# Attention and two feed-forward layers on one core: matmul kinds priced in the list schedule, a list of priority shifts, first loads in parts, TensorE warmed

## The chip, the cores and the metric

The kernel runs on one core of a Trainium2 chip. The metric is the time of one execution on the device in microseconds (us). It is a single program: all inputs come from HBM and the result goes back to HBM.

## What is computed

```python
# B, H, S, D = 4, 8, 576, 64
scores = q @ k^T / sqrt(D), causal mask, softmax    # per batch b and head h
local  = softmax @ v
q_p    = where(q > 0, q, exp(q) - 1) + 1
mem    = (q_p @ M_prev) / (q_p @ z_prev + 1e-6)
x      = g * mem + (1 - g) * local                  # g = sigmoid(beta) per head
x      = x as [2304 tokens, 512]
y      = (s * relu(x @ w_in)**2 + b) @ w_out        # first layers,  512 -> 2048 -> 512
h      = y @ w_in2                                  # second layers, 512 -> 2048 -> 512
out    = (max(h, 0) + alpha * min(h, 0)) @ w_out2
```

## The kernel before

The program is not written in the order in which it runs. `build` records operations (`op`): an engine, an estimated duration, the keys that it reads and writes, a priority, and a function that issues its instructions. `Plan.order` then makes a list schedule: it walks a model of the engines in time, and on each engine, when it is free, it takes the ready operation with the smallest priority number. The instructions are issued in that order, and each engine runs its own in order. The estimates therefore decide only the order; the waits on the chip are the real ones. Some operations (kind "x", in `either`) may go to ScalarE or to VectorE; the schedule gives them to the one that is free first.

The work has three parts. **Attention** goes by batch `b` and by pair of heads `p`: loads of q, k and v (`features` L526, `pair` L662, `values` L483), a feature map of q (L528, L529 on ScalarE, L532 on VectorE), matmuls with the memory (L549, normalised by L555 to L559), scores (L796), their row maximum (`largest`, L769, VectorE), exponentials (`exps`, L762, ScalarE), a scaling of the weights (batch 0: L579 on ScalarE or L581 on VectorE; later batches L630 and L634), a transposition (batch 0: on TensorE, L594, copied back by L602 on ScalarE or L604 on VectorE; later by DMA), and the outputs (L684, L700). The result of batch 0 is split into a high and a low part (L723 on ScalarE, L725 on VectorE), which the first layers read. `allone`, a tile of ones, is the weight of a small summing matmul (L499).

**The first layers** (`moe`) go by blocks of tokens, 512 in the first and 256 in the others, and by 16 slices `f` of the hidden width. `g1` makes one slice of the hidden layer in the bank `hb` with 12 matmuls (L928 to L930); ScalarE empties the bank (L941), squares (L942) and rounds (L943), VectorE makes the low part (L944), and `g2` multiplies with `w_out` (12 matmuls, L962 to L964). The weights of each slice are made while block 0 runs: a load (L880), three operations of VectorE (L882, L885, L888), a copy (L891) and a subtraction (L894). Batches 1 to 3 of the attention are interleaved with these layers.

**The second layers** (`hidden`, `output`) run when the attention is over: rows of matmuls of 384 columns (L1241 to L1243 and L1373 to L1375). At the very end `join` (L1256) adds the last bank to a kept part, and one DMA (L1389) stores 384 columns.

TensorE's matmuls have kinds: scores, turning (L594), outputs, memory, sum (L499) and layers. The schedule before adds 130 ns where a layer follows something else and 90 ns where something else follows a layer:

```python
layer = prio >= 10 ** 7
dur += 0 if layer == self.layer else 130.0 if layer else 90.0
```

All loads and stores are issued by SyncE's queue (SPq in the rows), in program order.

Of the kernel before, what the change touches and what calls it, by code (L numbers as in the profile page):

```python
# [20 lines left out]
NBIG, NB = 512, 256  # L21
NS, NTH = 384, NT // 2
# [36 lines left out]
KG = 1  # L59
# [5 lines left out]
WP = 1.7  # L65
TICK, WARM = 3413.3, 1275.0
# [19 lines left out]
class Plan:  # L86
# [8 lines left out]
    def __init__(self, nslots, nextra):  # L95
        self.nextra = nextra
        self.lean = 0
        self.ops = []
        self.ways = {}
        self.writer = {}  # L100
        self.readers = {}
        self.nslots = nslots
        self.layer = False

    def op(self, eng, dur, fn, r=(), w=(), prio=None, bytes_=0, claim=()):
# [16 lines left out]
        for k in list(r) + list(w):  # L122
            s = k[0] if isinstance(k, tuple) else k
            if isinstance(s, Slot) and s not in slots:
                slots.append(s)
                s.left += 1
        self.ops.append((eng, dur, fn, deps | late, i + self.lean if prio is None else prio, bytes_, slots, late, claim))
# [9 lines left out]
    def order(self):  # L137
        n = len(self.ops)
        left = [len(o[3]) for o in self.ops]
# [60 lines left out]
        gone = set()  # L200
        while len(out) < n:
# [88 lines left out]

def t_r(n):
    return 115.5 if n <= NB else (n + 32) / 2.4
# [31 lines left out]
def build(tc, kp, vd, qp, mzd, beta8, sb2, win1, wout1, win2, wout2, alpha, outT):  # L324
# [8 lines left out]
    with tc.tile_pool(name="sb", bufs=1) as sb, tc.tile_pool(  # L333
# [102 lines left out]
        def consts2():  # L436
# [6 lines left out]
        op("POOL", 200, lambda: nc.gpsimd.memset(allone, 1.0), w=["allone"])  # L443
        op("POOL", 200, lambda: nc.gpsimd.memset(ident, 1.0), w=["ident"])
        op("POOL", 500, lambda: nc.gpsimd.affine_select(
            out=ident, in_=ident, pattern=[[-1, 128]], compare_op=ALU.is_equal, fill=0.0, base=0, channel_multiplier=1),
           r=["ident"], w=["ident"])

# [7 lines left out]
        def bank_at(bk):  # L456
            return banks[bk.place - NSLOT - 3 * XF]

# [19 lines left out]
        def values(b, p, u, gs):  # L478
# [5 lines left out]
               r=gate(b, u, KV), prio=-7 if b + p == 0 else None, w=[sv], bytes_=512 * n)  # L484
# [9 lines left out]
            def part(x):  # L494
# [5 lines left out]
               r=[("tot", j), "allone"], w=[bk], prio=ATT + cnt["ch"] * 10 - 6)  # L500
# [15 lines left out]
        def features(b, p, u, gs):  # L516
# [4 lines left out]
            def cols(s):  # L521
# [945 lines left out]
```

## Time and profile before

| | |
|---|---|
| median of 3 runs | 937.06 us (937.0 to 938.16) |
| profiled execution, its time | 939.22 us |
| its span, first to last instruction | 937.2 us |
| TensorE busy | 921.1 us, 98% of the span |
| VectorE busy | 717.4 us, 77% |
| ScalarE busy | 604.6 us, 65% |

The span is that of the profiled execution, which lasted 2.0 us longer than its span. Busy time is a sum over the whole span; the stages differ, so the shares are read stage by stage. Matmuls overlap each other: the time from the start of one to the start of the next says more than the length of one.

### The profile page before, as it was taken

What the parts mean: (1) busy time and instruction counts of PE and PEld (TensorE: products, weight loads), DVE (VectorE), ACT (ScalarE), POOL (GpSimd) and SP (SyncE); (2) the same over time, 40 slices, a digit from 0 to 9 for tenths busy, and PEclk for the clock granted to TensorE, in tenths of its full rate; (3) what the DMA queues carried; (4) which work ended last, traced back from release to release, by engine and by line L of the source; (5) the groups of instructions that cost most, each with busy time, mean ns of one, the idle gap of its engine ahead of it and who ended that gap; (6) DMA issues with size and microseconds to landing.
All of it is one profiled execution on the core that took longest, in us unless ns stands there. A gap on an engine that the chain in (4) does not pass through costs nothing.

```text
span 937.2 us, 19293 instructions
## 1 busy us (share of the span) xinstructions
PE 921.1 (98%) x7164; PEld 845.2 (90%) x7164; DVE 717.4 (77%) x1636; ACT 604.6 (65%) x1413; POOL 5.3 (1%) x29
## 2 busy tenths in 40 slices
PE   7999999999999999999999999999999999999998
PEld 5677777688888888999999999999999999999998
DVE  6999998857777776647778767859568889786874
ACT  7887757767888888744544479748457665454452
POOL 1000000000000000000000000000000000000000
PEclk9999999999999999999999999999999999999999
DMA  4358955466766575567967746635348793725301
GB/s 158 98 144 254 284 180 166 124 139 128 183 146 148 121 168 109 90 185 253 323 228 281 257 156 218 210 111 165 115 133 271 231 306 117 238 68 163 107 1 68
DMA packets 154094, 160.43 MB, mean 171 GB/s; under 512 B 86928, under 2 KB 127888, under 8 KB 154000
## 3 DMA queue, kind: packets, MB, share of 16 engines
q1 hardware_dynamic: 154000, 159.20, 57.4%
q8 instruction: 56, 0.92, 0.4%
q14 instruction: 38, 0.31, 0.1%
HBM read 92.84 MB, written 46.66 MB: 149 GB/s over the span
## 4 chain that ended last, share of the span: by engine, by line
PE 83%; DVE 10%; ACT 3%; issue 2%; DMA 2%; SPq 0%; DVEq 0%; ACTq 0%
PE yb L962 6%; PE yb L964 6%; PE hb L928 6%; PE yb L963 6%; PE hb L929 6%; PE hb L930 6%; PE yb L1373 3%; PE sp L1374 3%; PE yb L1374 3%; PE sp L1373 3%; PE yb L1375 3%; PE sp L1375 3%; PE yb L1241 3%; PE yb L1243 3%; PE yb L1242 3%; PE sp L1243 2%
## 5 line engine op out<-in xcount | busy, mean ns | idle before, releaser
L962 PE MATMUL yb<-gr,wt 128*128 128x256 f32 (+2 forms) x512 | 154.5, 302 | 0.8 <-ACT gr L943 0.5
L928 PE MATMUL hb<-xr,wt 128*128 128x256 f32 (+1 forms) x512 | 152.9, 299 | 2.3 <-ACT gt L941 2.2
L964 PE MATMUL yb<-gr,wt 128*128 128x256 f32 (+2 forms) x512 | 151.5, 296 | 0.8 <-DVE gr L944 0.5
L930 PE MATMUL hb<-xr,wt 128*128 128x256 f32 (+1 forms) x512 | 149.7, 292 | 0.3 <-DVE wt L894 0.3
L929 PE MATMUL hb<-xr,wt 128*128 128x256 f32 (+1 forms) x512 | 149.7, 292 | 0.0
L941 ACT ACTIVATE gt<-hb 128x256 f32<-128x256 f32 (+1 forms) x128 | 52.3, 408 | 91.4 <-PE hb L930 76.9
L928 PEld LDWEIGHTS hb<-xr,wt 128*128 128x128 f32 x512 | 96.3, 188 | 11.3 <-issue 4.4
L962 PEld LDWEIGHTS yb<-gr,wt 128*128 128x128 f32 x512 | 96.3, 188 | 9.2 <-issue 3.7
L944 DVE TENSOR_TENSOR gr<-gt,gr 128x256 fp32r<-128x256 f32 (+1 forms) x128 | 58.3, 456 | 58.9 <-ACT gr L943 56.7
L964 PEld LDWEIGHTS yb<-gr,wt 128*128 128x128 f32 x512 | 96.9, 189 | 5.7 <-DVE gr L944 2.8
L930 PEld LDWEIGHTS hb<-xr,wt 128*128 128x128 f32 x512 | 96.7, 189 | 3.5 <-DVE wt L894 0.9
L929 PEld LDWEIGHTS hb<-xr,wt 128*128 128x128 f32 x512 | 96.3, 188 | 2.1
L963 PE MATMUL yb<-gr,wt 128*128 128x256 f32 (+2 forms) x320 | 93.8, 293 | 0.0
L963 PEld LDWEIGHTS yb<-gr,wt 128*128 128x128 f32 x320 | 60.3, 188 | 1.2
L943 ACT CAST gr<-gt 128x256 fp32r<-128x256 f32 (+1 forms) x128 | 55.3, 432 | 6.8 <-PE yb L963 4.4
L942 ACT ACTIVATE gt<-gt 128x256 f32<-128x256 f32 (+1 forms) x128 | 56.9, 445 | 2.8
L963 PE MATMUL yb<-gr,wu 128*128 128x256 f32 (+2 forms) x192 | 56.3, 293 | 0.0
L1198 ACT CAST xr<-spare 128x768 fp32r<-128x768 f32 x37 | 30.9, 836 | 26.6 <-PE sp L1374 10.1
L1267 ACT ACTIVATE waste<-poolx 128x384 f32<-128x384 f32 x48 | 25.2, 526 | 29.2 <-DVE poolx L1256 28.5
L1199 DVE TENSOR_TENSOR xr<-spare,xr 128x768 fp32r<-128x768 f32 x37 | 35.3, 955 | 9.6 <-ACT xr L1198 9.4
L963 PEld LDWEIGHTS yb<-gr,wu 128*128 128x128 f32 x192 | 36.1, 188 | 0.8
L1112 DVE TENSOR_TENSOR wp<-poolx,wp 128x768 fp32r<-128x768 f32 (+1 forms) x32 | 25.9, 822 | 8.9 <-ACT wp L1110 8.1
(505 smaller groups left out, 2570.2 us busy)
## 6 DMA issues: line engine op xcount, KB each, us to landing
g<-poolx SPq DMA_DIRECT2D x96, 192.0 KB, 1.9
poolu<-g SPq DMA_DIRECT2D x30, 384.0 KB, 4.2
room<-wout SPq DMA_DIRECT2D x14, 512.0 KB, 4.1
room<-win SPq DMA_DIRECT2D x13, 512.0 KB, 3.9
pool<-win SPq DMA_DIRECT2D x12, 512.0 KB, 4.6
pool<-wout SPq DMA_DIRECT2D x12, 512.0 KB, 5.0
spare<-y SPq DMA_DIRECT2D x12, 384.0 KB, 3.7
spare<-g SPq DMA_DIRECT2D x12, 384.0 KB, 3.6
```

What stands on the lines that cost most here:

```text
L928: T.matmul(H_, W_h, X_h, start=(d == 0), stop=False)
L929: T.matmul(H_, W_h, X_l, start=False, stop=False)
L930: T.matmul(H_, W_l, X_h, start=False, stop=(d == KD - 1))
L942: op("ACT", t_act(n), lambda: A.activation(out=t_, in_=t_, func=AF.Square), w=[tk], prio=-1)
L943: op("ACT", t_act(n), lambda: A.copy(out=G_h, in_=t_), r=[tk], w=[("gh", gj)], prio=-1)
L944: op("DVE", t_dve(n), lambda: V.tensor_tensor(out=G_l, in0=t_, in1=G_h.bitcast(F32), op=ALU.subtract), r=[tk, ("gh", gj)], w=[("gl", gj)], ...
L962: T.matmul(Y, W_h, G_h, start=first, stop=False, skip_group_check=True)
L963: T.matmul(Y, W_l, G_h, start=False, stop=False, skip_group_check=True)
L964: T.matmul(Y, W_h, G_l, start=False, stop=False, skip_group_check=True)
L1373: T.matmul(o, W_h, G_h, start=(m == e == 0 and P in (1, 2, 4, 5)), stop=False, skip_group_check=True)
L1374: T.matmul(o, W_l, G_h, start=False, stop=False, skip_group_check=True)
L1375: T.matmul(o, W_h, G_l, start=False, stop=False, skip_group_check=True)
```

## The change

Five edits. (1) Each TensorE operation now carries its kind, and `change` gives the price of each pair of kinds in the schedule's model, in place of the two numbers above. (2) `NUDGE`, a table of some 250 operations, shifts their priorities. (3) q and k of the first pair are loaded in two parts each (256 and 320 columns of q, 384 and 192 of k); the order of the first loads becomes q, k, q, k, beta, memory, v, where it was q, k, v, beta, memory. (4) `allone` is filled by VectorE at the start, and six matmuls of `allone` with itself run on TensorE before any load has landed (`begin`). (5) The last sum of the program is made and stored in two halves of 192 columns, one stored by SyncE's queue and one by ScalarE's.

```diff
+FIRST = 256, 384
+BEGIN = 6
+NUDGE = {
+    6: -10, 14: -16, 25: -2, 36: -437, 52: -1, 85: 27, 121: 5, 122: 5, 123: 5, 124: 9, 125: 5, 126: 5, 127: 5,
...
+    3340: 184, 3341: -1, 3392: 5, 3399: -36, 3433: -114, 3461: 1, 3473: -169, 3727: 282,
+}
...
     def order(self):
         n = len(self.ops)
+        for i, shift in NUDGE.items():
+            o = self.ops[i]
+            self.ops[i] = (*o[:4], o[4] + shift, *o[5:])
...
             if e == "PE":
-                layer = prio >= 10 ** 7
-                dur += 0 if layer == self.layer else 130.0 if layer else 90.0
-                self.layer = layer
+                dur += change(kind, self.kinds[i])
+                kind = self.kinds[i]
...
+def change(a, b):
+
+    if a is None:
+        return 0
+    if a == "scores":
+        return -89 if b == a else 0
+    if b == "scores":
+        return {"layers": 95, "outputs": 40}.get(a, 100)
+    if a == "outputs":
+        return {"layers": 75, "sum": 40, "outputs": 100}.get(b, 168)
+    if a == "sum":
+        return 140
+    return {"outputs": 9, "sum": 20}.get(b, 0) if a == "layers" else 0
...
 def t_r(n):
-    return 115.5 if n <= NB else (n + 32) / 2.4
+    return 116.4 if n <= NB else (n + 32) / 2.4
...
-        op("POOL", 200, lambda: nc.gpsimd.memset(allone, 1.0), w=["allone"])
+        op("DVE", 200, lambda: V.memset(allone, 1.0), w=["allone"], prio=-9)
+        bk0 = bank_for(0)
+
+        def begin():
+            for _ in range(BEGIN):
+                T.matmul(bank_at(bk0)[:, 0:128], allone, allone, start=True, stop=True)
+
+        op("PE", BEGIN * 4 * 128 / 2.4, begin, r=["allone"], w=[bk0], prio=-20, kind="memory")
...
-               r=gate(b, u, KV), prio=-7 if b + p == 0 else None, w=[sv], bytes_=512 * n)
+               r=gate(b, u, KV), prio=-5 if b + p == 0 else None, w=[sv], bytes_=512 * n)
...
-            op("SP", 475, lambda: nc.sync.dma_start(out=cols(sq), in_=qp[b, p][:, x0:x1_]),
-               r=gate(b, u, KV), prio=-9 if b + p == 0 else None, w=[sq], bytes_=512 * nx)
-            op("ACT", t_act(nx), lambda: A.activation(out=cols(se), in_=cols(sq), func=AF.Exp), r=[sq], w=[se])
+            for k, a, z in ((0, x0, FIRST[0]), (1, FIRST[0], x1_)) if b + p == 0 else ((0, x0, x1_),):
+                op("SP", 475, lambda a=a, z=z: nc.sync.dma_start(out=at(sq, S)[:, a:z], in_=qp[b, p][:, a:z]),
+                   r=gate(b, u, KV), prio=3 * k - 12 if b + p == 0 else None, w=[(sq, "b") if k else sq], bytes_=512 * (z - a))
+            op("ACT", t_act(nx), lambda: A.activation(out=cols(se), in_=cols(sq), func=AF.Exp), r=[sq, (sq, "b")], w=[se])
...
-            op("SP", 475, lambda: nc.sync.dma_start(out=at(sk, nkeys), in_=kp[b, p][:, 0:nkeys]),
-               r=gate(b, u, KG), prio=-8 if b + p == 0 else None, w=[sk], bytes_=512 * nkeys)
+            for k, a, z in ((0, 0, FIRST[1]), (1, FIRST[1], nkeys)) if b + p == 0 else ((0, 0, nkeys),):
+                op("SP", 475, lambda a=a, z=z: nc.sync.dma_start(out=at(sk, nkeys)[:, a:z], in_=kp[b, p][:, a:z]),
+                   r=gate(b, u, KG), prio=3 * k - 11 if b + p == 0 else None, w=[(sk, "b") if k else sk], bytes_=512 * (z - a))
...
-                    op("PE", t_p([y[6] for y in todo[::2]]), mm, r=[sqp, sk], w=keys + room_for, prio=ATT + (base + 2 * step[0]) * 10)
+                    op("PE", t_p([y[6] for y in todo[::2]]), mm, r=[sqp, sk] + [(s, "b") for s in (sqp, sk) if max(step) > 1],
+                       w=keys + room_for, prio=ATT + (base + 2 * step[0]) * 10, kind="scores")
...
+                                if (b, P, j) == (NTH // NS - 1, 2, 1):
+                                    for h, dma in enumerate((nc.sync, nc.scalar)):
+                                        x, n, c = NS // 2 * h, NS // 2, buf()
+
+                                        def add(c=c, x=x, n=n, k=kept[part, j]):
+                                            V.tensor_tensor(out=see(c, F32, 0, n), in0=bank_of[bank[1]][:, x:x + n],
+                                                            in1=see(k, F32, x, n), op=ALU.add)
+
+                                        act(c, t_dve(n), add, r=[bank[j]] + kept[part, j].keys, prio=-1, eng="DVE")
+                                        op(("SP", "ACT")[h], 475, lambda c=c, x=x + tq, n=n, d=d, dma=dma: dma.dma_start(
+                                            out=outT[:, d, x:x + n], in_=see(c, F32, 0, n)), r=c.keys, bytes_=512 * n)
+                                    continue
```

The edits move instructions on every engine from the first one on. Three places show how. The line numbers of the changed kernel are higher: its scores are L847 (L796 before), its maxima L820 (L769), its features L582 (L532), its constants L479 to L481 (L437 to L439), its layers L980 to L982 and L1014 to L1016 (L928 to L930 and L962 to L964).

The first place is the start of VectorE's stream. Before, the features of q and the three constants made from beta (`wsc`, `wlc`, `bgc`) stand ahead of the first maximum:

```order
L532 SCALAR_TENSOR_TENSOR room_73<-room_73,room_72 128x576
L437 TENSOR_SCALAR wsc<-wsc 128x36
L438 TENSOR_SCALAR wlc<-wsc 128x36
L439 TENSOR_SCALAR bgc<-bgc 128x36
L769 ISA sp_106,mx<-sp_106,mask 128x256
L769 ISA mx 128x1
L769 ISA sp_107,mx<-sp_107,mask 128x256
L769 ISA mx 128x1
L555 SCALAR_TENSOR_TENSOR nrm<-yb_101,bgc 128x4
```

In the changed kernel VectorE begins with the tile of ones and takes one maximum ahead of the features:

```order
L495 MEMSET allone 128x128
L820 ISA sp_107,mx<-sp_107,mask 128x256
L820 ISA mx 128x1
L582 SCALAR_TENSOR_TENSOR room_72<-room_72,room_71 128x576
L479 TENSOR_SCALAR wsc<-wsc 128x36
L480 TENSOR_SCALAR wlc<-wsc 128x36
L481 TENSOR_SCALAR bgc<-bgc 128x36
L820 ISA ob,mx<-ob,mask 128x256
L820 ISA mx 128x1
L820 ISA hb,mx<-hb,mask 128x384
L820 ISA mx 128x1
```

One maximum has moved ahead of the features and the constants, and the normalisation of the memory's result (L555 before) has moved behind further maxima.

The second place is on TensorE where the first layers begin, from the last group of slice f=0 (weights `wt_481`) to the first of slice f=1 (`wt_792`). Before, nothing stands between them:

```order
L928 MATMUL hb<-xr,wt_481 128x512
L929 MATMUL hb<-xr,wt_481 128x512
L930 MATMUL hb<-xr,wt_481 128x512
L928 MATMUL hb<-xr,wt_792 128x512
L929 MATMUL hb<-xr,wt_792 128x512
L930 MATMUL hb<-xr,wt_792 128x512
```

In the changed kernel (`wt_489`, then `wt_687`) a pair of scores of the attention stands between the two slices:

```order
L548 MATMUL sp_107<-vsc,allone 128x1
L980 MATMUL hb<-xr,wt_489 128x512
L981 MATMUL hb<-xr,wt_489 128x512
L982 MATMUL hb<-xr,wt_489 128x512
L847 MATMUL sp_106<-pool 128x384
L847 MATMUL ob<-pool 128x384
L980 MATMUL hb<-xr,wt_687 128x512
L981 MATMUL hb<-xr,wt_687 128x512
```

The scores moved to where the bank `hb` changes hands from one slice to the next.

The third place is on TensorE at the turn from block 0 to block 1, where the last `g2` of block 0 is followed by slice f=1 of block 1 (256 columns). Before, again nothing stands between:

```order
L962 MATMUL yb_104<-gr,wt_1759 128x512
L963 MATMUL yb_104<-gr,wt_1759 128x512
L964 MATMUL yb_104<-gr,wt_1759 128x512
L928 MATMUL hb<-xr,wt_792 128x256
L929 MATMUL hb<-xr,wt_792 128x256
L930 MATMUL hb<-xr,wt_792 128x256
```

In the changed kernel a pair of scores stands there:

```order
L1014 MATMUL yb_104<-gr,wt_1746 128x512
L1015 MATMUL yb_104<-gr,wt_1746 128x512
L1016 MATMUL yb_104<-gr,wt_1746 128x512
L847 MATMUL ob<-pool,poolx 128x512
L847 MATMUL sp_106<-pool,poolx 128x512
L980 MATMUL hb<-xr,wt_687 128x256
L981 MATMUL hb<-xr,wt_687 128x256
L982 MATMUL hb<-xr,wt_687 128x256
```

Counted over TensorE's whole stream, the runs of one kind are 189 before and 188 in the changed kernel, and the runs of layers among them 70 and 70.

## Rows read from the trace of the kernel before

**Rows 1.** Busy time by stage: length, busy us of each engine, PEclk, DMA.

```profile
0.00:4.57 4.57, 0.00 (x0) 0.03 (x1) 0.00 (x0) 2.13 (x3) 2.74 (x16) 1.00 0.59 192
4.57:16.00 11.43, 10.80 (x58) 7.29 (x60) 8.59 (x35) 7.80 (x25) 0.00 (x0) 1.00 0.60 204
16.00:64.00 48.00, 46.41 (x463) 34.00 (x464) 46.89 (x184) 44.26 (x143) 0.15 (x1) 1.00 0.32 103
64.00:176.00 112.00, 109.10 (x647) 81.42 (x646) 104.86 (x254) 75.94 (x165) 0.20 (x1) 1.00 0.72 208
176.00:560.00 384.00, 381.16 (x3779) 349.87 (x3779) 270.44 (x758) 257.27 (x698) 2.25 (x11) 1.00 0.66 181
560.00:933.70 373.70, 373.67 (x2224) 372.62 (x2222) 286.04 (x410) 217.19 (x384) 0.00 (x0) 1.00 0.49 158
933.70:937.20 3.50, 0.00 (x0) 0.00 (x0) 0.56 (x1) 0.00 (x0) 0.00 (x0) 0.88 0.31 112
```

**Rows 2.** Waits of TensorE, whole span: total us, times, longest.

```profile
PE sp L796 <- DMA room<-kp: 4.6, 1, 4.6
PE hb L928 <- ACT gt L941: 2.2, 2, 1.5
PE sp L499 <- DVE pool L559: 0.6, 1, 0.6
```

**Rows 3.** Waits of VectorE from 0 to 64 us.

```profile
DVE room L532 <- ACT room L529: 5.0, 1, 5.0
DVE wsc L437 <- ACT wsc L433: 1.4, 1, 1.4
DVE nrm L555 <- PE yb L549: 0.5, 1, 0.5
```

**Rows 4.** Timeline of the first 16 us: start, us, engine, line.

```profile
0.80 0.39 SPq L526 DMA_DIRECT2D room<-qp  x1
1.25 0.42 SPq L662 DMA_DIRECT2D room<-kp  x1
...
3.72 0.68 ACT L528 ACTIVATE room<-room 128x576 f32<-128x576 f32 x1 [1.64 <-DMA room<-qp]
...
4.57 1.22 PE L796 MATMUL sp<-room 64*128 64x256 f32 x4 [4.57 <-DMA room<-kp]
...
7.60 0.42 DVE L769 CUSTOM_DVE_ANT_0 sp<-sp,mask 128x256 f32<-128x256 f32 x1
...
7.70 2.51 PE L549 MATMUL yb<-mz,room 128*128 128x130 f32 x10 [0.63 <-DVE bgc L439]
...
14.46 0.61 PE L549 MATMUL yb<-mz,room 128*128 128x130 f32 x4
```

**Rows 5.** Groups of VectorE by shape, 0 to 66 us: busy us, mean ns.

```profile
L581 DVE TENSOR_SCALAR room<-room,sm 128x384 f32<-128x384 f32 x7 | 2.6, 415 | 0.0
...
L604 DVE COPY room<-yb 128x256 f32<-128x256 f32 x3 | 1.2, 414 | 0.0
...
L604 DVE COPY room<-yb 128x512 f32<-128x512 f32 x1 | 0.7, 692 | 0.0
...
L885 DVE SCALAR_TENSOR_TENSOR room<-pool,room 128x512 int32<-128x512 int32 x1 | 0.7, 693 | 0.0
```

**Rows 6.** Timeline of TensorE at the turn from block 0 to block 1.

```profile
183.72 0.38 PE L928 MATMUL hb<-xr,wt 128*128 128x256 f32 x1 [1.52 <-ACT gt L941]
```

**Rows 7.** Timeline of TensorE where scores follow layers.

```profile
317.03 0.28 PE L963 MATMUL yb<-gr,wt 128*128 128x256 f32 x1
317.15 0.28 PE L964 MATMUL yb<-gr,wt 128*128 128x256 f32 x1
317.35 0.69 PE L796 MATMUL sp<-poolx,pool 64*128 64x512 f32 x1
```

**Rows 8.** The last sum, in the timeline.

```profile
933.70 0.56 DVE L1256 TENSOR_TENSOR waste<-hb,waste 128x384 f32<-128x384 f32 x1 [0.49 <-PE hb L1375]
```

**Rows 9.** DMA issues at the end: count, KB each, us from issue to landing.

```profile
out_t<-waste SPq DMA_DIRECT2D x1, 192.0 KB, 1.9
```

More of the change, by code (lines that the diff above doesn't have):

```diff
@@ L102, in __init__, with op @@
         self.nslots = nslots
-        self.layer = False
-    def op(self, eng, dur, fn, r=(), w=(), prio=None, bytes_=0, claim=()):
+        self.kinds = []
+    def op(self, eng, dur, fn, r=(), w=(), prio=None, bytes_=0, claim=(), kind=None):
         i = len(self.ops)
@@ L126, in op @@
                 s.left += 1
+        self.kinds.append(kind)
         self.ops.append((eng, dur, fn, deps | late, i + self.lean if prio is None else prio, bytes_, slots, late, claim))
@@ L200, in order @@
         gone = set()
+        kind = None
         while len(out) < n:
@@ L442, in build @@
         op("DVE", 200, consts2, r=["wsc", "bgc"], w=["wsc", "bgc"])
-        op("POOL", 200, lambda: nc.gpsimd.memset(allone, 1.0), w=["allone"])
[L444 to L447, printed above, removed]
         cnt = {"ch": 0}
@@ L457, in bank_at @@
             return banks[bk.place - NSLOT - 3 * XF]
+        op("DVE", 200, lambda: V.memset(allone, 1.0), w=["allone"], prio=-9)
[4 more added lines that the diff above has]
+        op("PE", BEGIN * 4 * 128 / 2.4, begin, r=["allone"], w=[bk0], prio=-20, kind="memory")
+        op("POOL", 200, lambda: nc.gpsimd.memset(ident, 1.0), w=["ident"])
+        op("POOL", 500, lambda: nc.gpsimd.affine_select(
+            out=ident, in_=ident, pattern=[[-1, 128]], compare_op=ALU.is_equal, fill=0.0, base=0, channel_multiplier=1),
+           r=["ident"], w=["ident"])
         def gate(b, u, ahead):
@@ L499, in values @@
             op("PE", 100, lambda: T.matmul(bank_at(bk)[:, 0:1], allone, tot, start=True, stop=True),
-               r=[("tot", j), "allone"], w=[bk], prio=ATT + cnt["ch"] * 10 - 6)
+               r=[("tot", j), "allone"], w=[bk], prio=ATT + cnt["ch"] * 10 - 6, kind="sum")
             op("DVE", 131, lambda: V.tensor_scalar(
@@ L552, in features @@
                 gk = "bgc" if b in WHOLE else ("gg", u % 2)
-                op("PE", n * t_f(MZ), mm, r=[se, "mz", gk], w=[bk], prio=ATT + cnt["ch"] * 10 - 5)
+                op("PE", n * t_f(MZ), mm, r=[se, "mz", gk], w=[bk], prio=ATT + cnt["ch"] * 10 - 5, kind="memory")
                 gg = (bgc[:, 9 * p:9 * p + 2] if b in WHOLE else vsc[:, u % 2, 4:6]).rearrange("p (o h) -> p o h", o=1).to_broadcast([128, n, 2])
@@ L594, in mm @@
                                 T.transpose(bank_at(bk)[:, 128 * i:128 * i + 128], p_c(128 * (k0 + i), 128), ident)
-                        op("PE", n * t_t(128), mm, r=wk + ["ident"], w=[bk], prio=ATT + ch * 10 + 1)
+                        op("PE", n * t_t(128), mm, r=wk + ["ident"], w=[bk], prio=ATT + ch * 10 + 1, kind="turning")
                         def p_t(k0, n=1, p_c=p_c):
@@ L706, in outputs @@
                    r=sum((turned[odd, c][0] for turned, c in every for odd in range(2)), []) + [(sa, g) for g, _, _, _ in sets] + [sv, "ident"],
-                   w=list(oks.values()), prio=ATT + sets[0][2] * 10 + 2)
+                   w=list(oks.values()), prio=ATT + sets[0][2] * 10 + 2, kind="outputs")
                 for g, cs, _, _ in sets:
@@ L934, in g1 @@
                     ks_ = [(x, s, e) for x in ("xh", "xl") for s in range(2) for e in range(KD)]
-                op("PE", 3 * t_r(n), mm, r=wkeys("wi", f) + ks_ + [("xset", xs)], w=["H"], prio=MOE + cm["m"])
+                op("PE", 3 * t_r(n), mm, r=wkeys("wi", f) + ks_ + [("xset", xs)], w=["H"], prio=MOE + cm["m"], kind="layers")
             cm["m"] += 1
@@ L967, in g2 @@
                    w=[yk, ("g2", f)] + ([(yslot[d], "y")] if d in yslot else []),
-                   prio=MOE + cm["m"] + (1.5 if n == NBIG else 0))
+                   prio=MOE + cm["m"] + (1.5 if n == NBIG else 0), kind="layers")
             cm["m"] += 1
@@ L1243, in mm @@
                     T.matmul(o, W_l, X_h, start=False, stop=False, skip_group_check=True)
-            op("PE", t_s(NS), mm, r=[ready(P, f)] + XP(P, b).keys, w=[bank] + [("end", P)] * (g + 1 == len(GROUPS)), prio=MOE + cm["m"])
+            op("PE", t_s(NS), mm, r=[ready(P, f)] + XP(P, b).keys, w=[bank] + [("end", P)] * (g + 1 == len(GROUPS)), prio=MOE + cm["m"], kind="layers")
             cm["m"] += 1
@@ L1377, in output @@
                             op("PE", len(js) * t_s(NS), mm, r=[ready(P, 2 * m + e) for e in range(2)] + dst.keys, w=[bank[j] for j in js],
-                               prio=MOE + cm["m"])
+                               prio=MOE + cm["m"], kind="layers")
                             cm["m"] += 1
@@ L1386, in output @@
                                 c = buf()
+                                d, tq = j + 2 * (q % 2), t0 + NTH * (q // 2)
+                                if (b, P, j) == (NTH // NS - 1, 2, 1):
[8 more added lines that the diff above has]
+                                    continue
                                 join(bank[j], kept[part, j], c)
-                                d, tq = j + 2 * (q % 2), t0 + NTH * (q // 2)
                                 op("SP", 475, lambda c=c, d=d, tq=tq: nc.sync.dma_start(out=outT[:, d, tq:tq + NS], in_=see(c)),
```

2 lines of the change are left out of this document (1 added, 1 removed), and 17 rows, old and new, of the table NUDGE.

## Prediction

> **What bounds the kernel now.** I read the busy time by stage first, then the waits of TensorE, then the opening's timeline. In the stages the reader is to see who is full. From 560 to 933.7 us TensorE is busy 373.67 of 373.70 us [rows 1]: nothing but matmuls in steady order, and no edit touches what they do. From 176 to 560 us it is busy 381.2 of 384 us. From 64 to 176 us TensorE (109.1 of 112) and VectorE (104.9) are both nearly full, because VectorE makes the weights of the first layers there. From 16 to 64 us VectorE is busy 46.9 and ScalarE 44.3 of 48 us: this stage, attention of batch 0, ends when those two have done their work, and TensorE only waits for them in between. Ahead of 16 us nobody is full: VectorE does 8.6 us of work in 16.
>
> So time can come out in three places: an opening that ends earlier (what follows is full and moves forward as a whole), single waits of TensorE between 64 and 560 us, and the end behind the last matmul. The waits of TensorE that the profile names are few [rows 2]: 4.6 us for the first k, 2.2 us in two waits for the bank `hb`, 0.6 us for a sum; the rest are of 0.6 us and less.
>
> **Opening, the start.** VectorE idles 5.0 us for the first features, 1.4 us for the constants made from beta, and 0.5 us for the memory's matmuls: 6.9 us in all [rows 3]. The first q is issued at 0.80 and used at 3.72, the first k is issued at 1.25 and used by TensorE at 4.57 [rows 4]; both have 288 KB (128 rows of 576 floats), so a transfer that queues behind another costs 0.85 us per 288 KB, 0.34 MB per us. From that I estimate the parts: q's first 128 KB at 3.72 less 160 KB, 3.25 us; k's first 192 KB 0.56 us later, 3.8 us; the second parts at 4.3 and 4.6 us. The first scores can start at 3.8 and not at 4.57. The feature map needs both parts of q and starts at 4.3 where it started at 3.72: this is a loss of 0.6 us on ScalarE.
>
> The six matmuls of ones lie ahead of 3.8 us, where TensorE has nothing to do (first row of [rows 1]). A matmul of this kind is recorded twice; at the opening's pace of 0.22 us (below) twelve records take 2.6 us, from about 1.1 to 3.7 us. If VectorE's fill is late, the first scores are late by as much; with 0.1 us of room the cost is 0 to 0.3 us.
>
> What the warming buys: L549 at 7.70 us takes 2.51 us for ten, and at 14.46 us 0.61 us for four [rows 4]. Without the tail of the last one (0.55 and 0.28 us) that is 0.22 and 0.11 us from start to start, a factor of two, the ratio of the clock's two levels of 1.2 and 2.4 GHz, although the granted clock of the stage reads 1.00 in both [rows 1]. The slow pace still held 3 us after TensorE's first matmul. With the ones the work begins 3.5 us earlier. The scores of the first chunk then take between 1.2 us (the first four at 4.57, nothing gained) and 0.6 us, so the first maximum can start between 4.4 and 5.0 us. TensorE: Matmul & The Clock Gate of the Trainium skill, section What's actually happening, says that the clock is slow by default and activity releases it; by that rule alone the earlier value would hold. TensorE does not set the end of this stage, so the rule moves the sum by 0.6 us at most.
>
> VectorE's chain, worked out: maximum 4.7 to 5.2; features, which wait for ScalarE (4.3 plus twice 0.7), 5.7 to 6.5; the constants, whose beta no longer queues behind v (320 KB, 0.94 us), 6.5 to 7.0; second maximum at 7.0 us, where the first started at 7.60 [rows 4] and the second about 0.4 us behind it. That is 1.0 us, and the wait of 0.5 us for the memory goes, since seven more maxima stand ahead of its result. I take 1.5 us; bounds 0.5 (k's second part or beta later) and 2.3 us (fast pace at once).
>
> The page DMA: Bandwidth & Descriptors of the Trainium skill, section Rules for kernel authors, tells against parts: many small transfers should be one large one, as most of a small one is overhead. Here the second load is used 0.85 us behind the first, not 2.9 us, so what is fixed overlaps [rows 4]. If each part paid it alone, the second part of q would land about 2 us later and eat the 1.5 us; I give this little weight.
>
> **Opening, the work.** I counted VectorE's instructions ahead of its last L725 (first layers' input complete) in both programs. Scaling and copying that either engine can do move to ScalarE: L581 of 384 columns 7 to 3 (four at 0.415), of 256 3 to 5 and of 128 2 to 4 (0.35 and 0.29 by the slope), L604 of 512 6 to 3 (0.69), of 256 5 to 2 (0.41), of 384 2 to 4 (0.55), L730 4 to 2 (0.2) [rows 5]. Sum: -1.66 +0.70 +0.58 -2.07 -1.23 +1.10 -0.40 = -3.0 us. Two maxima of 256 columns fewer (0.42 [rows 4] and a short read-out each) and one L634 fewer give about -1.7, one more normalisation and the fill of ones +0.8, and one more weight slice is finished ahead of this point, four instructions of 0.4 to 0.69 us [rows 5], +2.4. Net -1.5 us. ScalarE takes on about 3 us; it idles 64 - 2.1 - 7.8 - 44.3 = 9.8 us up to 64 us [rows 1], but in its busiest part less, so I take 1.0 of the 1.5 us. The extra slice is VectorE work gone from the next stage, in which it is full: worth 0 to 2.4 us, I take 0.5, because TensorE is as full.
>
> **Waits between 64 and 560 us.** Two are named in the order. Between f=0 and f=1 the bank wait (2.2 less 1.5, 0.7 us [rows 2]) is covered by a pair of scores of 384 columns, about 0.8 us: -0.7. At the turn to block 1 the wait of 1.52 us [rows 6] gets a pair of 512 columns in it, about 1.1 us (256 columns at the slow pace took 1.22 [rows 4]): -1.1. The sum's 0.6 us [rows 2] stands three layer matmuls later, 0.7 us: -0.5. Against that, in the changed order two slices stand back to back once more, in a late block (nothing between the last matmul of one and the first of the next): +0.7 by the same row, and two places with only 0.7 us between them, 0.1 each. Net -1.4 us. What the order does not tell, whether VectorE's and ScalarE's rows come in time, I take as 0; bounds +3 (two more waits like the longest) and -3 (all others gone).
>
> **Prices of kinds.** A change costs about 0.08 us: within layers 0.12 us from start to start, 0.20 us where scores follow [rows 7]. The runs of one kind are 189 and 188, those of layers 70 and 70. The prices remove no changes: 0, bounds 0.3 either way.
>
> **End.** The last sum takes 0.56 us [rows 8], its store lands 1.9 us after issue [rows 9]. Two halves of some 0.33 us one behind the other end 0.1 us later; the second store has 96 KB less, 0.28 us. Sum -0.2 us, bounds +0.3 and -0.4.
>
> **Sum.** -1.5 -1.0 -0.5 -1.4 -0.2 = -4.6 us. The profiled span of 937.2 becomes 932.6; the execution is 2.0 us longer, but the median of the runs shown is 937.06, so I set the sum against that: 932.5 us.
>
> **Rivals.** (a) ScalarE becomes the opening's bound. For it: 44.3 of 48 us busy and 3 us more. Against: it idles 9.8 us in all. The opening then yields 0.5 and the slice nothing: 935.0 us. (b) The new order removes nearly all named waits and VectorE's gain passes whole: opening 3.8, slice 1.5, waits 4.4, end 0.2: 927.2 us. For it: the two largest places are treated just so; against: waits are not only removed, one is added. (c) Slower: `hb` is emptied late. ScalarE runs a fixed order; where a row ahead of L941 has late input, the next slice waits as at 183.72 us, 1.52 us each [rows 6]. Four such places beyond the sum bring 938.6, five 940.1 us. It decides (over 0.2%) from five on. Against: before has one in 384 us. (d) The edits do not do what they say in sum: the opening's gain is lost again before 176 us, where two engines are full and a later load can be missing; with the waits' net 0: 936.9 us.
>
> **Chances.** My forecast, 930 to 934.8 us, 0.50; (a) 0.17; (b) 0.13; (d) 0.09; (c) 0.11. A measurement tells 0.2% from no change, 1.9 us. Faster: forecast, (b), and two thirds of (a), 0.74. Same: the rest of (a) and (d), 0.15. Slower: (c), 0.11. Range 927.5 to 937.0 us: it holds the forecast, (a), (d) and most of (b); the forecast's own is 930 to 934.8.
>
> **What would show it.** The first scores near 3.8 us and L549's pace of 0.11 us from its first group; the second maximum near 7 us; the first layer matmul near 61.5 us, where now it is at the border of two stages, 64 us; no wait for `hb` between f=0 and f=1, under 0.5 us at the turn to block 1, and one new wait of about 0.7 us in a late block; 560 us to the end as before. I am wrong if ScalarE is full up to 60 us, if the first layers start later than 63.5 us, or if waits for L941, L943 or L944 sum to more than 5 us.

## The result and the profile after

The changed kernel takes 928.5 us (median of 4 runs, 926.78 to 929.46), the kernel before 937.07 us beside it: ratio 0.9904, 95% interval 0.9887 to 0.9921. The forecast was 932.5 us, the range 927.5 to 937.0. The profiled execution of the changed kernel lasted 928.72 us, its span is 926.8 us, 10.4 us less than that of before; the medians differ by 8.6 us, as the profiled execution of before lay 2.2 us over its median.

The stages of the changed kernel, in the columns of [rows 1]; the cuts lie at its first scores (4.28), its first layer matmul (64.61) and its last matmul's end (923.6):

```profile
0.00:4.28 4.28, 2.94 (x13) 2.67 (x13) 0.17 (x1) 0.00 (x0) 2.53 (x14) 1.00 0.47 134
4.28:16.00 11.72, 10.57 (x58) 6.19 (x60) 9.13 (x41) 10.43 (x31) 0.00 (x0) 1.00 0.78 265
16.00:61.00 45.00, 41.93 (x416) 31.36 (x413) 42.36 (x164) 42.21 (x134) 0.31 (x2) 1.00 0.37 115
61.00:64.61 3.61, 3.59 (x53) 2.76 (x51) 3.60 (x13) 3.46 (x12) 0.00 (x0) 1.00 0.37 130
64.61:176.00 111.39, 111.39 (x675) 85.35 (x676) 106.78 (x266) 79.77 (x179) 0.20 (x1) 1.00 0.72 199
176.00:550.00 374.00, 373.49 (x3752) 345.78 (x3751) 268.37 (x745) 253.88 (x686) 2.26 (x11) 1.00 0.69 188
550.00:923.60 373.60, 373.53 (x2222) 372.26 (x2220) 284.30 (x406) 216.14 (x381) 0.00 (x0) 1.00 0.49 156
923.60:926.80 3.20, 0.00 (x0) 0.00 (x0) 0.62 (x2) 0.00 (x0) 0.00 (x0) 1.00 0.36 123
```

The opening is not shorter: the first layer matmul starts at 64.61 us, and at 64.28 us in the trace of before. From there to 176 us TensorE is busy without a hole (111.39 of 111.39), where it was 109.1 of 112 [rows 1]. The second layers take what they took (373.6 us for 2222 recorded matmuls, against 373.7 us for 2224), the end 3.20 in place of 3.50 us.

So the time came out between 64 and 550 us, from TensorE's waits. Of these the view of waits (from 66 to 925 us) names one in the changed kernel; before it named seven lines with 4.6 us in all, two of them in [rows 2].

```profile
PE hb L980 <- ACT gt L993: 0.5, 1, 0.5
```

4.6 us of named waits cannot give 10 us. The view counts only idle time behind the modelled end of a matmul, and a matmul is recorded some 0.17 us longer than its step. One place in the trace of before, TensorE's timeline at 403 us:

```profile
402.40 0.28 PE L962 MATMUL yb<-gr,wt 128*128 128x256 f32 x1
402.51 0.28 PE L963 MATMUL yb<-gr,wt 128*128 128x256 f32 x1
403.13 0.39 PE L964 MATMUL yb<-gr,wt 128*128 128x256 f32 x1 [0.34 <-DVE gr L944]
403.36 0.28 PE L962 MATMUL yb<-gr,wt 128*128 128x256 f32 x1
```

The steps are 0.11 us, here one is 0.62 and the next 0.23: 0.50 us are lost in the first step alone, and 0.34 are named. I counted all first-layer matmuls so: the start of the next matmul, less the own start, less the steady step (0.114 us for 256 columns, 0.227 for 512). Places at which the next one is late by 0.15 us or more, from each kernel's trace; the last column is half of the time that the trace shows at a granted clock of 0.50 ahead of the last matmul:

```
                            first layer   late      their    last matmul   missing
                            matmul, us    places    sum, us  ends, us      clock, us
before                      64.3          23         9.5     933.7         0
changed                     64.6           3         1.0     923.6         0
without the list            67.0           9         4.7     929.9         3.4
  and old prices            64.9          20        10.1     938.1         1.7
prices a tenth up, no list  64.7          15        10.1     939.8         3.4
before with new prices      66.4          26        12.0     943.0         3.4
list with old prices        72.4          34        15.1     947.3         8.5
list with signs turned      63.4          25        18.8     951.2         8.5
```

From before to changed this is 8.5 of the 10.4 us. The end gives 0.3, the opening takes 0.3; the other 1.9 us lie in delays under 0.15 us and in the pace of the second layers. In these two traces the clock stays at 1.00 up to the last matmul, in the six others it does not; at the lower clock each step is about twice as long (0.21 us for 256 columns at 329.5 us with the prices a tenth up), so a few late places there (12 of the 34 with list and old prices) are the clock's.

### The profile page after: what moved, and what is told of

Same layout as the page of the kernel before. It is cut to its first block, busy times and chain, and to the rows that moved or that the text cites. A ratio compares the mean times of both kernels' runs of the same rounds, so it can differ in the third digit from the quotient of the medians.

```text
span 926.8 us, 19360 instructions
## 1 busy us (share of the span) xinstructions
PE 917.4 (99%) x7176; PEld 846.4 (91%) x7176; DVE 715.3 (77%) x1634; ACT 605.9 (65%) x1417; POOL 5.3 (1%) x28
## 4 chain that ended last, share of the span: by engine, by line
PE 96%; DVE 2%; ACT 1%; issue 0%; DVEq 0%; ACTq 0%
PE hb L980 8%; PE yb L1014 8%; PE yb L1016 7%; PE yb L1015 7%; PE hb L982 7%; PE hb L981 7%; PE yb L1425 3%; PE yb L1426 3%; PE sp L1426 3%; PE yb L1427 3%; PE sp L1427 3%; PE sp L1425 3%; PE yb L1293 3%; PE yb L1295 3%; PE yb L1294 3%; PE sp L847 3%
## 5 line engine op out<-in xcount | busy, mean ns | idle before, releaser
L980 PE MATMUL hb<-xr,wt 128*128 128x256 f32 (+1 forms) x512 | 153.5, 300 | 0.5 <-ACT gt L993 0.5
L1014 PE MATMUL yb<-gr,wt 128*128 128x256 f32 (+2 forms) x512 | 152.9, 299 | 0.0
L1016 PE MATMUL yb<-gr,wt 128*128 128x256 f32 (+2 forms) x512 | 150.6, 294 | 0.0
L982 PE MATMUL hb<-xr,wt 128*128 128x256 f32 (+1 forms) x512 | 149.6, 292 | 0.0
L980 PEld LDWEIGHTS hb<-xr,wt 128*128 128x128 f32 x512 | 96.3, 188 | 8.3 <-issue 2.2
L1014 PEld LDWEIGHTS yb<-gr,wt 128*128 128x128 f32 x512 | 96.3, 188 | 7.3 <-issue 4.4
L1016 PEld LDWEIGHTS yb<-gr,wt 128*128 128x128 f32 x512 | 96.5, 189 | 3.3 <-DVE gr L996 0.5
L982 PEld LDWEIGHTS hb<-xr,wt 128*128 128x128 f32 x512 | 96.4, 188 | 2.6
L1425 PE MATMUL yb<-xr,wp 128*128 128x384 f32 x96 | 32.2, 335 | 0.0
```

The lines of the kernel that those rows point to most:

```text
L980: T.matmul(H_, W_h, X_h, start=(d == 0), stop=False)
L982: T.matmul(H_, W_l, X_h, start=False, stop=(d == KD - 1))
L1014: T.matmul(Y, W_h, G_h, start=first, stop=False, skip_group_check=True)
L1016: T.matmul(Y, W_h, G_l, start=False, stop=False, skip_group_check=True)
L1425: T.matmul(o, W_h, G_h, start=(m == e == 0 and P in (1, 2, 4, 5)), stop=False, skip_group_check=True)
```

## The experiments

Each ratio is to the kernel before, run beside it.

### The list and the prices

**Without the list.** The loop over the list runs over nothing:

```diff
-        for i, shift in NUDGE.items():
+        for i, shift in ():
```

> The changed kernel with the table of priority shifts emptied; prices, opening and tail stay. Theory 'list' (the shifts removed the short waits inside the runs of layers): the waits inside layer runs from 56 us on return from 5.9 to about 14 us and the time is 935 to 938 us. Theory 'prices' (the price per pair of kinds did it): the waits stay near 6 us and the time is 928 to 930 us. Theory 'opening' (the prediction's, a good half of the gain before 64 us): 930 to 931 us.

Measured: 933.92 us (931.68 to 937.47, 12 runs), ratio 0.9964 (0.9953 to 0.9976). That lies between the theories 'prices' and 'list'; 'opening' is out. The list is worth 5 to 6 us on top of the rest. Four of the 12 executions have a mean granted clock of 0.996 to 0.998; the other eight have a median of 933.3 us, still 4.8 us above the changed kernel.

**Without the list and with the two prices of before.** As above, and:

```diff
-                dur += change(kind, self.kinds[i])
+                layer = self.kinds[i] == "layers"
+                dur += 0 if layer == (kind == "layers") else 130.0 if layer else 90.0
```

> As the one before, and the two old prices (130 and 90 ns) as well, so that only the opening and the tail of the change are left. Theory 'list' and theory 'prices' agree that nothing but the tail is left, 936.5 to 938 us; theory 'opening' says 934 to 935 us. Between this kernel and the one before lies what the prices do: 0 by 'list', 6 to 8 us by 'prices'.

Measured: 945.03 us, ratio 1.0081 (1.0068 to 1.0094). No theory had said more than 938 us. What is left of the change is the opening, the ones, the halves and the new estimate of a layer matmul (`t_r`, 116.4 for 115.5 ns, never tried alone); with the two prices of before they give an order that is slower than before.

**The prices alone.** The kernel before, with the table `change`, the kinds and the new estimate `t_r`, and nothing else of the change:

```diff
-                layer = prio >= 10 ** 7
-                dur += 0 if layer == self.layer else 130.0 if layer else 90.0
+                dur += change(kind, self.kinds[i])
+                kind = self.kinds[i]
```

> The kernel before with the price table and its kinds alone: no list, no parts, no warming, no halves at the end. Prices alone: the two runs so far without the list differ by 11.1 us in the price table (933.9 and 945.0). If the table itself makes the order good, the kernel before gains the like: inner and exit waits of the layer runs fall from 18.8 us to about 12.7, the sum that the run without the list showed, and the time is 929 to 932. If the two prices of before are as good as the table, and the 945.0 was one unlucky order among many, the time is 935 to 940.

Measured: 943.25 us (941.4 to 948.75), ratio 1.0069 (1.0046 to 1.0091), slower than either theory said. The table is not better than the two prices as such.

**Every price a tenth up, without the list.**

```diff
-        for i, shift in NUDGE.items():
+        for i, shift in ():
...
-                dur += change(kind, self.kinds[i])
+                dur += 1.1 * change(kind, self.kinds[i])
```

> The run without the list (933.9 us) with every price of the table raised by a tenth: a change without meaning, to see how far orders scatter by chance. If the table's prices are right and what they bring is no luck: within 2 us of 933.9. If the order is one of many and the time is chance: outside, anywhere from 928 to 946.

Measured: 944.71 us (943.47 to 947.76), ratio 1.0083 (1.0065 to 1.0102). This is what the theory of chance said: a change without meaning costs 10.8 us against 933.9. The four largest of its waits of TensorE behind 66 us (without the list no single wait is over 0.9 us):

```profile
PE hb L980 <- ACT xr L1073: 3.4, 1, 3.4
PE yb L1016 <- DVE gr L996: 2.0, 3, 0.8
PE hb L1293 <- DVE poolx L1308: 1.8, 1, 1.8
PE hb L980 <- ACT gt L993: 0.7, 2, 0.5
```

Each is an input that ScalarE or VectorE made late. Behind the longest, a stall of 3.6 us from start to start at 324.8 us, the granted clock falls:

```profile
325.00:330.00 5.00, 1.61 (x7) 1.40 (x6) 1.99 (x6) 2.03 (x9) 0.00 (x0) 0.74 0.89 289
330.00:335.00 5.00, 4.61 (x25) 4.18 (x24) 3.89 (x17) 3.59 (x13) 0.21 (x1) 0.58 0.01 2
```

That costs up to 3.4 us more. It is no accident of one execution: all six have a mean clock of 0.993 to 0.996.

**The list with the old prices.** The edit of the prices as in the second run, the list kept.

> The changed kernel with the list, but with the two prices of before in place of the table. If the list is good for itself: about 11 us less than without it (945.0 us), 932 to 936. If list and prices only fit together, each shift being measured against one order: no better than 945, up to 955.

Measured: 954.75 us (952.49 to 956.5), ratio 1.0187 (1.0169 to 1.0204): 9.7 us more than without the list, as the theory said by which list and prices only fit together.

**The list with its signs turned.**

```diff
-        for i, shift in NUDGE.items():
+        for i, shift in ((i, -x) for i, x in NUDGE.items()):
```

> The changed kernel with every shift of the list turned to the other sign. If the list carries knowledge of the waits (each shift placed by what the chip did), turning it gives as much as having none or worse: 933.9 us or more, up to 940. If any stir of the order does as well (the order without a list being an unlucky one), the time stays at 927 to 931.

Measured: 957.22 us (954.15 to 958.14), ratio 1.0203 (1.0185 to 1.0221), 17 us above the highest that was expected. The four largest of its waits behind 66 us:

```profile
PE hb L980 <- ACT gt L993: 4.7, 6, 2.1
PE yb L548 <- ACT poolx L546: 4.0, 1, 4.0
PE yb L1014 <- ACT gr L995: 2.8, 3, 2.1
PE hb L1293 <- DVE poolx L1308: 2.4, 1, 2.4
```

The six runs together: the shifts help in the order that the price table makes, where they take 5.4 us away; in the order of the old prices, the only other one tried, the same list adds 9.7 us. The prices act through the order that they happen to give: with 70 to 73 runs of layers in all of these kernels, the times go from 928.5 to 957 us. Not all of that is waiting. Of the 28.7 us up to the list with its signs turned, up to 8.5 are missing clock: its trace has four stretches at 0.50, each behind a late input of 2 to 4 us, and its five executions have mean clocks of 0.989 to 0.993 (0.987 to 0.991 with the list and the old prices).

### The opening

In the changed kernel ScalarE's and VectorE's first rows are these (timeline):

```profile
1.12 2.93 PE L500 MATMUL sp<-allone 128*128 128x128 f32 x12 [1.12 <-DVE allone L495]
4.28 0.76 PE L847 MATMUL sp<-room 64*128 64x256 f32 x1 [0.22 <-DMA room<-kp]
4.64 1.28 ACT L578 ACT_TABLE_LOAD   x1 [4.64 <-DMA room<-qp]
5.93 0.68 ACT L578 ACTIVATE room<-room 128x576 f32<-128x576 f32 x1
7.22 0.76 DVE L582 SCALAR_TENSOR_TENSOR room<-room,room 128x576 f32<-128x576 f32 x1 [1.10 <-ACT room L579]
8.29 0.43 DVE L820 CUSTOM_DVE_ANT_0 ob<-ob,mask 128x256 f32<-128x256 f32 x1
```

ScalarE loads the table of its exponential (1.28 us) behind the wait for both parts of q. So the features start at 5.93 us, not at 4.64, and the second maximum at 8.29.

**The table first.** A tiny exponential of the tile of ones stands ahead of the first features:

```diff
-        sb.tile([128, 16], F32, name="lead")
+        pre = sb.tile([128, 16], F32, name="lead")[:, 0:2]
...
-            op("ACT", t_act(nx), lambda: A.activation(out=cols(se), in_=cols(sq), func=AF.Exp), r=[sq, (sq, "b")], w=[se])
+            def expq(first=b + p == 0):
+                if first:
+                    A.activation(out=pre, in_=allone[:, 0:2], func=AF.Exp)
+                A.activation(out=cols(se), in_=cols(sq), func=AF.Exp)
+
+            op("ACT", t_act(nx), expq, r=[sq, (sq, "b")], w=[se])
```

> The changed kernel with one more instruction: a tiny exponential of two columns of ones at the head of ScalarE's stream, so that the table load no longer stands behind the wait for q. Everything else in the same order. Theory 'late table' (the opening's gain was lost to the 1.28 us table load behind the load of q): features start at 4.65 and not 5.93 us, the first layer matmul 0.8 to 1.3 us earlier than 64.6 us, time 927.2 to 927.8 us. Rival 'full engines' (ScalarE is full from 10 to 62 us, other waits take it): features earlier, first layer within 0.3 us of 64.6, time 928.2 to 928.8 us.

Measured: 926.92 us (925.75 to 928.98, 4 runs), ratio 0.9891 (0.9876 to 0.9906). Its timeline:

```profile
0.80 1.28 ACT L580 ACT_TABLE_LOAD   x1 [0.80 <-PEq L1529]
4.71 0.68 ACT L581 ACTIVATE room<-room 128x576 f32<-128x576 f32 x1 [2.41 <-DMA room<-qp]
7.06 0.43 DVE L825 CUSTOM_DVE_ANT_0 ob<-ob,mask 128x256 f32<-128x256 f32 x1
```

The features start 1.22 us earlier, the second maximum 1.23, the first layer matmul 1.26 (63.35 against 64.61). That is the theory 'late table': in the trace the table load is the whole of it. The time is 1.6 us lower, but the intervals of the two kernels' ratios overlap.

**Whole loads.** q and k of the first pair are loaded whole in the place of their first parts; the second parts issue nothing:

```diff
-                op("SP", 475, lambda a=a, z=z: nc.sync.dma_start(out=at(sq, S)[:, a:z], in_=qp[b, p][:, a:z]),
+                op("SP", 475, lambda a=a, z=z, k=k: k or nc.sync.dma_start(out=at(sq, S)[:, x0:x1_], in_=qp[b, p][:, x0:x1_]),
... (k in the same way)
```

> The changed kernel with q and k of the first pair loaded whole, each at the place of its first part; all else in the same order. If ScalarE is the bound of the opening and the table load waits for all of q: q lands at 3.7 and not 4.6, ScalarE's first features start at about 5.0 in place of 5.93, the time is 0.9 below, 927.5 to 928.0. If the parts pay (first scores at 4.28 and not 4.6): 928.6 to 929.5.

Measured: 926.11 us (925.32 to 929.23, 4 runs), ratio 0.9883 (0.9865 to 0.9901). Its timeline:

```profile
0.80 1.28 ACT L578 ACT_TABLE_LOAD   x1 [0.80 <-PEq L1524]
3.59 0.68 ACT L578 ACTIVATE room<-room 128x576 f32<-128x576 f32 x1 [1.51 <-DMA room<-qp]
4.55 0.45 PE L847 MATMUL sp<-room 64*128 64x256 f32 x1 [0.50 <-DMA room<-kp]
4.84 0.38 PE L847 MATMUL sp<-room 64*128 64x256 f32 x1
6.79 0.43 DVE L820 CUSTOM_DVE_ANT_0 ob<-ob,mask 128x256 f32<-128x256 f32 x1
```

I expected the table load behind the wait here too; it stands at 0.80 us by itself. Where the first exponential waits for two loads the table load came behind the wait, where it waits for one it came ahead. The features gain 2.34 us, the first scores lose 0.27, and the first layer matmul starts at 63.19 us.

The page ScalarE: Activation LUTs of the Trainium skill, section What ACT_TABLE_LOAD costs, gives 1283 ns for the load and 1380 ns for a drain beside it; the 1.28 us agree, of a drain these rows show nothing: the features start 0.01 us behind the load's end.

**Both.** The table first and whole loads.

> The changed kernel with both: a tiny exponential of the tile of ones ahead of the first features, which takes the table load out of their way, and q and k loaded whole. If ScalarE's first features set the opening, they start at 3.7 and not 4.71 as with the table load first alone (926.9 us): 925.9 to 926.3, the first layer matmul at about 62.4 us. If the opening hangs on the first scores (4.6 and not 4.28): 927.0 to 927.5.

Measured: 926.71 us (925.68 to 930.6, 6 runs), ratio 0.9893 (0.9874 to 0.9912); four runs lie at 925.7 to 926.9 us, two at 930.1 and 930.6, and these two have a mean granted clock of 0.996 (the next run shows what that is). The median lies between the two theories, the four at full clock are near the first. With whole loads the tiny exponential moves nothing: the features start at 3.59 us with and without it.

**No warming.** `begin` issues no matmuls:

```diff
-            for _ in range(BEGIN):
-                T.matmul(bank_at(bk0)[:, 0:128], allone, allone, start=True, stop=True)
```

> The changed kernel in the same order, without the six matmuls of ones. Theory 'warming does not pay here' (VectorE waits for the features until 7.2 us anyway): slow pace of the first scores, second maximum not later than 8.6 us, time 928.3 to 929 us. Theory of the prediction (0 to 0.6 us): 928.5 to 929.1 us. If warming were the opening's main gain: 930 us or more.

Measured: 929.58 us (928.61 to 930.71, 4 runs), ratio 0.9918 (0.9905 to 0.993). That is above the two forecasts that end at 929.1 us and below the 930 us of a warming that is the opening's main gain. Its first layer matmul starts at 66.9 us, 2.3 us later. But the opening is not where that is lost. These are windows of its trace:

```profile
46.00:48.00 2.00, 0.88 (x6) 0.67 (x6) 2.00 (x10) 2.00 (x7) 0.00 (x0) 1.00 0.00 0
48.00:50.00 2.00, 2.00 (x12) 1.80 (x10) 1.61 (x7) 1.52 (x7) 0.00 (x0) 0.54 0.00 0
50.00:52.00 2.00, 1.48 (x7) 0.79 (x5) 1.62 (x7) 1.90 (x6) 0.00 (x0) 0.50 0.01 4
52.00:54.00 2.00, 2.00 (x19) 1.88 (x21) 1.86 (x9) 1.88 (x6) 0.00 (x0) 0.50 0.00 0
54.00:56.00 2.00, 2.00 (x32) 1.93 (x30) 0.11 (x1) 0.48 (x2) 0.00 (x0) 0.75 0.00 0
```

The granted clock is 0.50 (1.2 GHz) for about 7 us, behind 2 us of which TensorE was busy 0.88 us. ScalarE and VectorE, full until then, have nothing to do at 54 us. The missing clock sums to 3.4 us.

### The gap at 46 us

The gap is in the changed kernel too (waits of TensorE, 40 to 50 us):

```profile
PE yb L644 <- ACT poolx L813: 1.1, 1, 1.1
PE yb L644 <- ACT pool L629: 0.4, 1, 0.4
```

Its profiled execution kept the clock at 1.00 behind it, although TensorE was busy for only 0.57 us from 46 to 48 us. Of the 22 executions of kernels in this order (changed, table first, whole loads, both, no warming) 8 have a mean granted clock of 0.998 or less, 3 of the 4 without warming among them. Two of the eight were traced ("Both" and "No warming"), and in both traces the clock falls at 48 us.

**The gap filled.** Whole loads, and at this place one transposition is repeated seven times into the same place:

```diff
+                            more.append(n)
+                            if sum(more) == 61:
+                                for _ in range(7):
+                                    T.transpose(bank_at(bk)[:, 0:128], p_c(128 * k0, 128), ident)
```

> The changed kernel with q and k of the first pair whole (926.1 us alone), and one more thing: where TensorE stands idle for 1.1 us at about 45 us, one transposition of 128x128 is repeated seven times into the same place. In the changed order some executions show a granted clock of 0.50 for about 7 us behind this gap and take 3 to 4 us longer (926.1 us is the median of 925.3, 925.7, 926.6 and 929.2), others do not. If the gap is what lets the clock fall: none of the runs shows a mean clock below 0.999 and the times lie at 925.3 to 926.6. If the fall comes from elsewhere: one run in three stays at 929 or above.

Measured: 927.87 us (926.2 to 929.23, 6 runs), ratio 0.9893 (0.9877 to 0.991); no mean clock is below 0.999. Two windows of its trace, ahead of and behind the place:

```profile
44.00:48.00 4.00, 3.32 (x26) 2.11 (x23) 4.00 (x21) 4.00 (x14) 0.00 (x0) 1.00 0.02 7
48.00:54.00 6.00, 5.43 (x67) 4.62 (x67) 5.67 (x22) 6.00 (x21) 0.00 (x0) 1.00 0.01 1
```

**The gap filled, without warming.** The same repetition, in the kernel whose `begin` issues nothing.

> The changed kernel without the six matmuls of ones (929.6 us; three of its four runs with the clock's fall at 48 us) and with the same repeated transposition in the gap. If what the missing warming cost was that fall: 926.5 to 928.0, as the changed kernel in its undisturbed runs. If the warming is worth something at the start itself: 928.5 and more, with no fall at 48 us.

Measured: 928.15 us (926.94 to 928.92, 5 runs), ratio 0.9898 (0.9883 to 0.9913); all mean clocks 1.0. That is the changed kernel's time, with no matmul of ones, but between the two forecasts: above 928.0 and below 928.5 us.

In 11 executions with the gap filled the clock never fell, in 22 without it fell in 8. That speaks for the gap as the cause, and for this fall as most of the price in the run without warming: the one of its executions without a fall took 928.61 us. But the time did not follow as I expected: 927.9 us is no better than 926.1, the runs with a full clock still scatter from 926.2 to 929.2 us. The traces of the two kernels with whole loads show where: with the gap filled the last matmul ends 3.2 us later (923.3 against 920.1 us). The first layer matmul starts 0.8 us later (63.99 us), and TensorE has two waits behind 66 us that the other trace does not have:

```profile
PE yb L1022 <- DVE gr L1002: 0.6, 1, 0.6
PE sp L1433 <- DVE xr L1257: 0.5, 1, 0.5
```

Each costs 0.7 us from start to start: VectorE's row came late in one execution and not in the other. Why it was late, and whether the filled gap has a part in it, stays open. At the start, the second pair of scores starts 0.29 us behind the first with whole loads, 0.56 with the gap filled (4.49 and 5.05 us), with the same instructions ahead of it and a granted clock of 1.00 in both. The page TensorE: Matmul & The Clock Gate of the Trainium skill, section What's actually happening, says that the number of slow matmuls at a start varies from run to run of one kernel; these traces, of two kernels that are alike up to there, agree.

No version is shown to beat the changed kernel: whole loads has the lowest ratio, 0.9883, and its interval overlaps that of the change. Both beat the kernel before.

## Why the prediction was right in sum and wrong in its steps

**What bounds it** held: 550 us to the end unchanged, the gain inside 64 to 550 us possible because TensorE is full there.

**Opening, the start (-1.5): failed, 0.** The step by which the feature map "starts at 4.3" left the table load out. Before it ran at 0.80 us under the load of q; the parts put it behind the wait. With it moved the second maximum starts at 7.06 us; 7.0 was forecast. The first scores came at 4.28 and not 3.8 us; without the ones they start at 3.94. That would be a delay of 0.3 us by the ones, which end at 4.05, the upper end of what I allowed. But q's second part, too, was used at 4.35 us without the ones and at 4.64 with them, so the loads themselves may have landed later; the cause is not shown. The second part of q came 0.3 us later than the 4.3 that I told, not the 2 us of parts that each pay the fixed time alone. The second pair of scores starts 0.55 us behind the first with the ones and 0.56 without: nothing was gained there. The pace of 0.11 us came from the first group of the memory's matmuls, but without the ones as well (six in 0.83 us both times), so it is no sign of the warming. What the warming buys was nothing that 928.15 against 928.5 us shows (the former has the gap filled too); the bound of "0.6 us at most" holds.

**Opening, the work (-1.0 and -0.5): failed, about 0.** VectorE's work up to the first layer fell by 0.2 us (55.3 against 55.5), ScalarE's rose by 1.9 (56.1 against 54.2; sums over the first three rows of [rows 1] and the first four above). Windows of the changed kernel:

```profile
16.00:20.00 4.00, 4.00 (x40) 2.31 (x37) 2.82 (x11) 4.00 (x14) 0.00 (x0) 1.00 0.39 97
20.00:30.00 10.00, 9.81 (x115) 8.54 (x115) 9.37 (x39) 10.00 (x34) 0.15 (x1) 1.00 0.29 97
30.00:62.00 32.00, 29.12 (x280) 21.27 (x278) 31.16 (x121) 29.21 (x92) 0.15 (x1) 1.00 0.42 132
```

ScalarE is full from 16 to 30 us, and VectorE waits there: rival (a) as to the opening. Of the three signs that I named as "I am wrong if" one came, first layers later than 63.5 us; one came in part, ScalarE full up to 30 us and not 60; the waits of more than 5 us did not come. Even with the start mended the first layers begin at 63.2 us and not at 61.5.

**Waits (-1.4): right places, wrong size, about -8.5.** The three places came as told: no wait between f=0 and f=1, none at the turn to block 1 where 1.52 us stood, none for the sum. The new wait of two slices back to back is there, in a late block:

```profile
536.84 0.28 PE L982 MATMUL hb<-xr,wt 128*128 128x256 f32 x1
537.59 0.39 PE L980 MATMUL hb<-xr,wt 128*128 128x256 f32 x1 [0.47 <-ACT gt L993]
```

0.75 less the step of 0.11 is 0.64 us; 0.7 was forecast. What failed is the sentence "bounds ... -3 (all others gone)". It sized the pool by the named waits, 4.6 us; start to start it held 9.5 us in 23 places, and the changed kernel has 3 with 1.0 us. That is rival (b)'s mechanism, nearly all waits gone, with twice its price and without its opening.

**Prices of kinds (0, bounds 0.3 either way): failed as a bound.** The count behind it was right: entering a run of layers costs 6.8 us in sum in both kernels (the first two steps of each of the 70 runs, less the steady ones). But the prices also decide which order comes out, and that moved the time by about 6 us up when they and `t_r` were the only edits, and by 11 us down beside the other edits. Neither the row that I read nor the count could tell this.

**End (-0.2): right,** 0.3 by the trace; the halves were not tried alone. TensorE's last row, and what follows:

```profile
923.23 0.34 PE L1427 MATMUL hb<-xr,wp 128*128 128x384 f32 x1
923.60 0.62 DVE L1445 TENSOR_TENSOR waste<-hb,waste 128x192 f32<-128x192 f32 x2 [0.48 <-PE hb L1427]
924.25 0.38 ACTq L1449 DMA_DIRECT2D out_t<-waste  x1
```

The second store is issued as late as the one store was before (0.65 us behind the start of the sum, 0.59 before), and the span ends 2.55 us behind it; it was 2.91.

So 932.5 against 928.5 us is an opening that gave nothing of its 3.0 us, and waits that gave about 7 us more than their term. Two errors of opposite sign brought the time into the range, below the forecast's own 930 to 934.8 us: that is luck.

## What to carry to other kernels

Size a full engine's waits from start to start, not by the named idle time: short stalls hide behind modelled ends, and here they were half of the pool. A table of shifts found for one order belongs to that order: with the prices of another order it did harm here, so after such an edit it has to be made again; and a price table has to be judged by several orders, since a tenth on every price moved the time without the list by 10.8 us, more than the whole gain. A late input can cost twice, by the wait and by the clock that falls behind it: the granted clock belongs beside the waits when two orders are compared. When a first load is split, look at what stood under it: here a table load of 1.28 us slipped behind the second part.

## What the runs showed of the hardware

- ScalarE's table load (1.28 us) stood at 0.80 us when the first exponential waited for one load, and behind the wait, at 4.64 us, when it waited for two.
- Behind a stretch (46 to 48 us) of which TensorE was busy 0.80 and 0.88 us, the granted clock was 0.50 for about 7 us in two traces, 3.4 us of clock lost each time; in the changed kernel's trace it stayed at 1.00 although TensorE was busy there for 0.57 us only. Of 22 executions 8 show such a loss in their mean clock; with seven more transpositions in the gap none of 11 does.
- In two orders with late inputs of 2 to 4 us in the layers the trace has the clock at 0.50 behind them, 3.4 us lost with the prices a tenth up and 8.5 with the list's signs turned; every execution shows the like in its mean clock (0.993 to 0.996, and 0.989 to 0.993).
- With six matmuls of ones ahead of them each time and a granted clock of 1.00, the second pair of scores started 0.55 us behind the first (changed) and 0.56 (gap filled), but 0.29 with whole loads.
